# A long convolution with a gated block behind it: the order of the last chunks of the fourth stage, and when two half loads go out

## The chip, the cores and the metric

The kernel runs on 1 core of a Trainium2 chip, all in float32. The metric is device time in microseconds (us) of one launch, the median of several runs. Engines are named as in the profile: PE (TensorE, with PEld its weight loads), DVE (VectorE), ACT (ScalarE), POOL (GpSimd), SP (SyncE, here only a DMA queue).

## The reference, cut to what matters

```python
# x (8, 6400, 128), h (6400, 128); _attn_ref, then _moe_ref on its result
L = 2 * S
y = np.fft.irfft(np.fft.rfft(x, n=L, axis=1) * np.fft.rfft(h, n=L, axis=0)[None], n=L, axis=1)[:, :S]
xp = np.concatenate([np.zeros((B, K - 1, D)), y], axis=1)              # K = 5 taps
gate_pre = sum(conv_w[k] * xp[:, k:k + S] for k in range(K))
out = (1 / (1 + np.exp(-gate_pre))) * (y @ w_val) @ w_out
```

So: a causal convolution of length 6400 for each of 128 channels, then a gate from a 5-tap filter of its result, a product with a projection, and a second projection.

## The kernel before, in words

The long convolution is done by transforms written as matrix products. For each of the 8 batches there are four stages (matmuls are counted as the trace has them, two for each in the code). The first (`Forward`) makes sums and differences of the input on POOL (`sums`, two instructions of 128x256) and multiplies them (`half`, 32 matmuls into two banks of PSUM, which ACT copies away). The second (`Product`) transforms on and multiplies with the spectrum of h, which is loaded in blocks from DRAM into four buffers `h_sb`. The third (`s3_quads`, here s3(g)) has 16 groups g of 64 matmuls; ACT copies part of the result (`keep`, `ends`) and DVE joins it into the tile `dt` with two instructions (`join`). The fourth (`Chunk.s4`) makes the convolution's result in 13 chunks of the 64 columns; a chunk is named by its first column: 60 (four columns), 0, 5, ... 55 (five each).

Batches overlap. The third stage of batch b runs with the first stage of batch b + 1 and with what is left of the chunks of batch b - 1; the fourth stage of batch b runs with the second stage of batch b + 1. The order on every engine is the program's own (`keep_in_program_order`), so an instruction that waits holds all that stand behind it on its engine.

What a chunk c does, under the names of this document:

- s4(c): 40 matmuls into one of four banks of PSUM (`single`; the pool `ps1` has four). The planner gives a bank that is free to the next tile that asks, the one that was freed longest ago; a tile asks when its first matmul comes.
- y(c): an ACT copy of the chunk to SBUF. "Late" chunks (25 to 55 where a batch follows) do nothing else here: their bank is free behind that copy, and their filter is done in the next third stage.
- The other chunks (0, 5, 10, 15, 20) do their filter now, from the bank: `init` and `keep` on ACT, then taps(c) on DVE (taps 0, 1 and 2, each adds into five columns, c + j to c + j + 4; some in two pieces), and add(c) on POOL, which adds the buffer that `keep` filled to columns c + 3 to c + 7. The bank is free when taps(c) are done.
- project(c) (PE), the sigmoid (ACT), gate(c) (DVE), output(c) (PE), store: for 0 and 5 in the fourth stage, for the others in the third stage of the next batch, in the groups that `VALUE` and `OUTPUT` name, late chunks' taps in groups 2k and 2k + 1 with k = (c - 25) / 5.

The fourth stage is a loop over steps s; step s emits, in this order, project of the jobs that are due, s4 of chunk number s, output of the jobs of the step before, ACT's copies for chunk number s, the taps of chunk number s - 1, the add of chunk number s - 2, and the gate of the jobs:

```python
            if 0 < s <= NCH and not cs[s - 1].late:
                cs[s - 1].taps()
            if 2 < s < NCH + 2 and not cs[s - 2].late:
                cs[s - 2].add()
            for c in jobs[s]:
                c.gate()
```

and in steps 9 and 10 of all batches but the last two the first two `sums` of the next first stage (sums(0) and sums(1)); group g of the third stage then emits s3(g), half(g), sums(g + 2), and what is due of the chunks. The second stage has ended on PE by step 8, so steps 9 to 12 hold the last four chunks alone; this document calls them the tail.

Before, the chunks go 60, 0, 35, 40, 45, 50, 55, 5, 10, 15, 20, 25, 30. The buffers that `keep` fills are four, `keeps`: two tiles `p_t` and the two halves of `h_sb[0]`, the latter for chunks 15 and 20 (and for 5). The first block of the spectrum for the next second stage is loaded into the same two halves, on ACT's queue, from the third stage (`ahead`, in the groups that `AHEAD` names); such a load must wait until the add that reads the half is done.

Of the kernel before, what the change touches and what calls it, by code (L numbers as in the profile page):

```python
# [30 lines left out]
CH = 5  # L31
HEAD = (60, 4)
CHUNKS = [HEAD] + [(a, CH) for a in range(0, 60, CH)]
NCH = len(CHUNKS)
OUT_ORDER = CHUNKS[1:] + [HEAD]
LATE = 35
HELD = 10
# [6 lines left out]
XH = 8  # L44
VALUE = {10: 0, 15: 1, 20: 2, 25: 4, 30: 5, 35: 6, 40: 8, 45: 10, 50: 12, 55: 14}
OUTPUT = {10: 2, 15: 3, 20: 4, 25: 6, 30: 7, 35: 8, 40: 9, 45: 11, 50: 13}
AHEAD = {
    0: (1, 0, 0), 1: (1, 0, 1), 4: (0, 0, 0), 5: (0, 0, 1), 7: (1, 1, 0), 8: (0, 1, 0),
    9: (0, 1, 1), 10: (0, 2, 0), 11: (0, 2, 1), 12: (1, 1, 1), 13: (1, 2, 0), 14: (1, 2, 1),
}  # L50

# [78 lines left out]
def longconv_moe(ctx: ExitStack, tc: tile.TileContext, x, h, r1, m2, r3, m4, w64, out):  # L130
# [34 lines left out]
    p_t = [cp.tile([128, CH, N1], F32, name=f"p_{i}") for i in range(2)]  # L165
    keeps = p_t + [h_sb[0][:, i : i + CH * N1].rearrange("p (n t) -> p n t", t=N1) for i in (0, BL // 2)]
# [70 lines left out]
    def single():  # L237
        return ps1.tile([128, 512], F32, name="pt1", tag="pt1")
# [66 lines left out]
    def ahead(spectrum, kb, half):  # L305
        i = half * SB // 2
        if spectrum:
            k = slice(2 * C * i, 2 * C * i + SB * C)
            nc.scalar.dma_start(h_sb[kb % HB][:, k], hd[kb, :, k])
        else:  # L310
            j = kb * SB + i
            nc.scalar.dma_start(m2_sb[kb % M2B][:, i : i + SB // 2], m2[:, j : j + SB // 2])
# [58 lines left out]
    def s3_quads(d0):  # L371
        pt = pair()
        for q in range(4):
            for c in range(2):
                for r, k in ((0, 0), (1, 0), (1, 1), (0, 1)):
                    d, o = k * HP + d0 + q, (r + k) % 2
                    w = d // 2 * 2 * N1 + c * 2 * HR + d % 2
                    v = pt[o * HP : (o + 1) * HP, k, q * 2 * N2 : (q + 1) * 2 * N2].rearrange("p (b m) -> p b m", b=2)
                    nc.tensor.matmul(
                        v[:, :, c::2],  # L380
                        lhsT=gyf[r * HP : (r + 1) * HP, w : w + 2 * HP - 1 : 2],
                        rhs=r3_sb[r * HP : (r + 1) * HP, c, :],
                        start=True,
                        stop=True,
                    )
        v = pt.rearrange("p k (d b m) -> p b m k d", b=2, m=N2)
        a = d0 // 4 % 2 * 512
        t = h_sb[HB - 1][:, a : a + 512]
        o = dv.rearrange("p n c (k d) -> p (n c) k d", k=2)[:, :, :, d0 : d0 + 4]

        def keep():
            act(
                t.rearrange("p (m c d) -> p m c d", c=2, d=2 * XG)[:, :, ::-1],
                pt.rearrange("p k (d b m c) -> p b m c (k d)", b=2, m=N2 // 2, c=2)[:, 1],
            )

        def join(op, n):
            u = t.rearrange("p (m k d) -> p m k d", k=2, d=XG)
            nc.vector.tensor_tensor(out=n, in0=v[:, 0, 2:], in1=u[:, 2:], op=op)

        def ends():
            act(o[:, 0:2], v[:, 0, :2])
            act(o[:, N2 : N2 + 2], v[:, 1, :2])

        return keep, ends, lambda: join(ADD, o[:, 2:N2]), lambda: join(ALU.subtract, o[:, : N2 + 1 : -1])
# [26 lines left out]
    class Chunk:  # L432
# [51 lines left out]
                self.p = self.y  # L484

        def keep(self):
            self.q = p_t[(self.ch[0] - HELD) // CH % 2] if self.late else keeps[(self.i + (self.i // 8 if self.defer else 1)) % 4]
            self.first(3, self.q, self.p)
            if self.r is not None:
                self.first(2, self.r, self.p)  # L490
# [95 lines left out]
    def m4_load(j, half=None):  # L586
        a = CH * j, CH * j + CH + (j == 12)
        if half is not None:
            a = (a[0] + 2 * half, a[1] if half else a[0] + 2)
        a = slice(*a)  # L590
        nc.sync.dma_start(m4_sb[:, a], m4.rearrange("k (n t) -> k n t", t=MW)[:, a])
# [28 lines left out]
    for b in range(B):  # L620
        nxt = b + 1 < B


        steps = collections.defaultdict(list)
        for c in pend:
            a = c.ch[0]
            if a == HEAD[0]:
                t = NS - 1
            else:
                t = VALUE[a]  # L630
            if c.late:
                k = (a - WAIT) // CH
                if not nxt:
                    c.r = rows[k % 3]
                steps[2 * k] += [lambda c=c: c.taps(range(2))]
                steps[2 * k + 1] += [lambda c=c: c.taps(range(2, 4)), c.add]
            steps[t] += [c.project]
            steps[t if a in OUTPUT else NS - 1] += [c.sigm, c.gate]
            if a in OUTPUT:
                steps[OUTPUT[a]] += [c.output]  # L640
                steps[OUTPUT[a] + 1] += [c.store]
        pend = [c for c in pend if c.ch[0] in (HEAD[0], HEAD[0] - CH)]
        for g in range(NS):
            e = s3_quads(4 * g)
            f = []
            if nxt:
                f = fx.half([single(), single()])
                fx.sums(nc.gpsimd)
            for u in e:
                u()  # L650
            if nxt and g in AHEAD:
                ahead(*AHEAD[g])
            for u in f:
                u(act)
            if b == 0:
                next(wgen, None)
                next(wgen, None)
                if g < 8:
                    m4_load(m4_rest[0], g % 2)
                    if g % 2:  # L660
                        m4_rest.pop(0)
            for u in steps[g]:
                u()
        if nxt:
            h_load(HB - 1)
        if b + 2 < B:
            fx = Forward(x[b + 2], gy)


        chs = CHUNKS if not nxt else sorted(CHUNKS, key=lambda c: (c != HEAD, c[0] > 0, c[0] < LATE))  # L670
        cs = [Chunk(b, i, ch, nxt) for i, ch in enumerate(chs)]
        jobs = collections.defaultdict(list)
        for i, c in enumerate(cs):
            if i and not c.late and not c.held:
                jobs[i + 3].append(c)
        if not nxt:
            jobs[NCH + 2].append(cs[0])
        pr = {}

        def s2(kb):  # L680
            if nxt and kb < NKB:
                pr[kb] = Product(kb)
                m2_load(kb + M2B)

        def times(kb):
            if kb in pr:
                pr[kb].mul_u()
                pr[kb].mul_t()
                pr.pop(kb).add()
                h_load(kb + HB)  # L690

        outs, at = [], 0
        for s in range(max(NCH, *jobs) + 2):
            kbs = list(range(at, min(at + 2 - s % 2, NKB))) if nxt else []
            at += len(kbs)
            if s == 0:
                s2(0)
                s2(1)
            if s < 2:
                cs[s].s4()  # L700
            late = pend[s : s + 1]
            if late and s == 0:
                late[0].output()
            for kb in kbs[:1]:
                if kb:
                    s2(kb + 1)
            if m4_rest:
                m4_load(m4_rest.pop(0))
            for c in jobs[s]:
                c.project()  # L710
            if 1 < s < NCH:
                cs[s].s4()
            for c in outs + late[: s]:
                c.output()
            for c in jobs[s]:
                c.sigm()
            for kb in kbs[:1]:
                times(kb)
            for kb in kbs[1:]:
                s2(kb + 1)  # L720
            if s < NCH:
                cs[s].copies()
            for c in outs + late:
                c.store(p_t[0][:, : c.ch[1]] if s == 0 or nxt and c.ch[0] == CH else None)
            for kb in kbs[1:]:
                times(kb)
# [6 lines that stand above are left out]
            outs = jobs[s]  # L733
            if b + 2 < B:
                if s == 5:
                    fx.load(XB)
                if s in (9, 10):
                    fx.sums(nc.gpsimd)
        pend = [cs[0]] + [c for c in cs if c.held or c.late]
# [45 lines left out]
```

## Time and profile before

| | |
|---|---|
| median of 3 runs | 947.44 us (945.7 to 949.0) |
| the profiled execution | 948.98 us, its span 947.2 us |
| PE, DVE, POOL, ACT busy | 861.0, 746.1, 580.3, 511.4 us |
| mean granted clock of PE | 0.986 |
| one period (third and fourth stage) | about 108 us |

The span runs from the first to the last instruction on the core; the time holds some 1.8 us around it. Busy time is the union of an engine's instructions. There are seven seams from a fourth to a third stage where a batch follows (at 201, 309, 416, 524, 635, 742 and 851 us); the change touches each of them. The last fourth stage, at 893 us, keeps its order.

### The profile page before, as it was taken

The numbers are of one execution on the slowest core, as the hardware profiler recorded it, in microseconds if no ns is written. First come the engines' busy times: TensorE is split into PE (matmuls) and PEld (weight loads), VectorE is DVE, ScalarE is ACT, GpSimd is POOL, SyncE is SP. The second block draws the span as 40 slices with busy tenths as digits, with TensorE's granted clock in tenths as the row PEclk, the third lists the DMA queues.
The fourth block names the chain that finished last, engine by engine and source line by source line (L and its number), as shares of the span: only waits on it lengthen the run. The fifth ranks groups of instructions, "written<-read, shape, count | busy, mean of one in ns | idle before, by whom it ended". The sixth has DMA issues, their size and how long they took to land. (4 is left out here: it accounts for less than half of the span.)

```text
span 947.2 us, 48024 instructions
## 1 busy us (share of the span) xinstructions
PE 861.0 (91%) x21360; PEld 687.3 (73%) x21360; DVE 746.1 (79%) x1041; ACT 511.4 (54%) x1222; POOL 580.3 (61%) x602
## 2 busy tenths in 40 slices
PE   7799668998999999999899989999999898999897
PEld 6699658965688658975688657875589666985563
DVE  5546757887898879888797867879888787979785
ACT  4522443277624784178624765157733685248776
POOL 5446744776477765867477754876558664764332
PEclk9899799999999999999999999999999999999999
DMA  7776646926584566925594455935576365921112
GB/s 251 261 256 240 205 153 233 341 81 174 171 312 156 152 199 204 317 82 175 168 307 155 131 188 173 334 105 160 178 266 234 104 200 153 316 92 47 66 56 96
DMA packets 79406, 177.42 MB, mean 187 GB/s; under 512 B 14048, under 2 KB 27360, under 8 KB 79200
## 3 DMA queue, kind: packets, MB, share of 16 engines
q1 hardware_dynamic: 67104, 152.33, 48.0%
q10 hardware_dynamic: 12096, 22.03, 8.0%
q8 instruction: 168, 2.75, 1.2%
q14 instruction: 38, 0.31, 0.1%
HBM read 141.56 MB, written 32.77 MB: 184 GB/s over the span
## 5 line engine op out<-in xcount | busy, mean ns | idle before, releaser
L117 POOL TENSOR_TENSOR gy<-gy,ring 128x512 f32<-128x512 f32 (+1 forms) x182 | 220.6, 1244 | 104.5 <-DVE ring L117 52.4
L117 PEld LDWEIGHTS pt<-r_sb,gy 64*64 64x64 f32 x8192 | 143.8, 138 | 105.2 <-issue 66.9
L117 DVE TENSOR_TENSOR dt<-pt,ring 128x496 f32<-128x496 f32 x256 | 159.8, 667 | 66.3 <-ACT dt L117 63.2
L117 PEld LDWEIGHTS pt<-m_sb,dt 128*64 128x64 f32 x4096 | 184.8, 136 | 28.8 <-issue 12.7
L117 POOL TENSOR_TENSOR sd<-x 128x256 f32<-128x256 f32 x236 | 183.3, 806 | 28.2 <-issue 13.4
L117 PE MATMUL pt<-m_sb,dt 128*64 128x100 f32 x4096 | 192.6, 248 | 7.7 <-DVE ring L117 6.4
L117 PE MATMUL pt<-gy,ring 128*64 128x128 f32 x3008 | 187.3, 278 | 9.2 <-PE pt L117 4.2
L117 ACT COPY ring<-pt 128x512 f32<-128x512 f32 (+2 forms) x216 | 129.2, 601 | 119.6 <-PE pt L117 58.9
L117 PEld LDWEIGHTS pt<-gy,ring 128*64 128x64 f32 x3008 | 174.5, 135 | 21.4 <-PE pt L117 8.0
L117 PE MATMUL pt<-r_sb,gy 64*64 64x64 f32 x8192 | 163.2, 227 | 17.5 <-issue 12.2
L117 PE MATMUL pt<-r_sb,sd 50*64 50x100 f32 x4608 | 144.8, 260 | 33.3 <-issue 25.8
L117 DVE TENSOR_TENSOR gy<-pt,ring 128x1024 f32<-128x1024 f32 (+1 forms) x99 | 117.0, 1182 | 52.5 <-PE pt L117 50.6
L117 PEld LDWEIGHTS pt<-r_sb,sd 50*64 50x64 f32 x4608 | 120.3, 142 | 39.6 <-issue 29.8
L117 DVE TENSOR_TENSOR ring<-pt,ring 128x1024 f32<-128x1024 f32 (+2 forms) x131 | 134.6, 1028 | 11.3 <-PE pt L117 2.4
L117 ACT COPY gy<-pt 128x400 f32<-128x400 f32 x248 | 110.6, 500 | 36.3 <-PE pt L117 35.1
L117 ACT COPY yl<-pt 128x500 f32<-128x500 f32 (+1 forms) x89 | 51.2, 575 | 125.8 <-PE pt L117 125.7
L117 POOL TENSOR_TENSOR gl<-gl,p 128x500 f32<-128x500 f32 (+1 forms) x46 | 54.1, 1177 | 105.9 <-DVE gl L117 69.4
L117 ACT COPY dt<-pt 128x16 f32<-128x16 f32 (+2 forms) x310 | 62.7, 254 | 72.8 <-PE pt L117 72.7
L117 DVE SCALAR_TENSOR_TENSOR gl<-yl,w_sb,gl 128x500 f32<-128x500 f32 (+1 forms) x107 | 91.9, 864 | 3.1 <-ACT gl L117 1.1
L117 PE MATMUL pt<-ring,w_sb 128*64 128x500 f32 x320 | 81.5, 604 | 3.2 <-DVE ring L117 3.1
L117 DVE SCALAR_TENSOR_TENSOR ring<-pt,w_sb,ring 128x500 f32<-128x500 f32 (+3 forms) x94 | 63.1, 671 | 5.7 <-ACT ring L117 1.3
L117 POOL TENSOR_TENSOR ring<-ring,p 128x500 f32<-128x500 f32 (+1 forms) x24 | 25.2, 1051 | 46.8 <-DVE ring L117 22.8
(62 smaller groups left out, 795.5 us busy)
## 6 DMA issues: line engine op xcount, KB each, us to landing
ring<-m SPq DMA_DIRECT2D x69, 512.0 KB, 5.8
ring<-hd SPq DMA_DIRECT2D x63, 512.0 KB, 5.1
x<-xl SPq DMA_DIRECT2D x118, 256.0 KB, 3.5
ring<-hd ACTq DMA_DIRECT2D x42, 256.0 KB, 3.3
ring<-m ACTq DMA_DIRECT2D x42, 256.0 KB, 3.8
out<-ring SPq DMA_DIRECT2D x40, 250.0 KB, 3.9
out<-yl SPq DMA_DIRECT2D x40, 250.0 KB, 4.0
hd<-ring SPq DMA_DIRECT2D x8, 512.0 KB, 4.1
```

What stands on the lines that cost most here:

```text
L117: return self._tc.keep_in_program_order(call(*args, **kwargs))
```

## The change: another order of six chunks, and two loads two groups later

The order of the chunks becomes 60, 0, 35, 40, 45, 50, 55, 5, 10, 25, 15, 20, 30, written out as `ORDER`: the late chunk 25 moves ahead of 15 and 20. The buffers of `keep`, which went by a chunk's number in the order, are written out by its column (`KEEP`). The two half loads of the spectrum's first block move from groups 0 and 1 of the third stage to groups 2 and 3. As the rest of a chunk's work goes through the list in the new order, chunk 25 also comes before 15 and 20 in each group of the third stage.

```diff
+ORDER = (60, 0, 35, 40, 45, 50, 55, 5, 10, 25, 15, 20, 30)
+KEEP = {0: 1, 5: 3, 10: 1, 15: 2, 20: 3}
 AHEAD = {
-    0: (1, 0, 0), 1: (1, 0, 1), 4: (0, 0, 0), 5: (0, 0, 1), 7: (1, 1, 0), 8: (0, 1, 0),
+    2: (1, 0, 0), 3: (1, 0, 1), 4: (0, 0, 0), 5: (0, 0, 1), 7: (1, 1, 0), 8: (0, 1, 0),
     9: (0, 1, 1), 10: (0, 2, 0), 11: (0, 2, 1), 12: (1, 1, 1), 13: (1, 2, 0), 14: (1, 2, 1),
 }
...
         def keep(self):
-            self.q = p_t[(self.ch[0] - HELD) // CH % 2] if self.late else keeps[(self.i + (self.i // 8 if self.defer else 1)) % 4]
+            a = self.ch[0]
+            if self.late:
+                self.q = p_t[(a - HELD) // CH % 2]
+            else:
+                self.q = keeps[KEEP[a] if self.defer else (self.i + 1) % 4]
...
-        chs = CHUNKS if not nxt else sorted(CHUNKS, key=lambda c: (c != HEAD, c[0] > 0, c[0] < LATE))
+        chs = CHUNKS if not nxt else [(a, CH) if a < HEAD[0] else HEAD for a in ORDER]
```

## Rows read from the trace of the kernel before

**Rows 1.** The page, part 1: busy time, share of the span and instructions of each engine.

```profile
PE 861.0 (91%) x21360; PEld 687.3 (73%) x21360; DVE 746.1 (79%) x1041; ACT 511.4 (54%) x1222; POOL 580.3 (61%) x602
```

**Rows 2.** Busy time in one fourth stage (first row) and the third stage behind it: stretch, its length, then busy time (and instructions) of PE, PEld, DVE, ACT, POOL, the granted clock, the DMA share and GB/s.

```profile
148.05:201.45 53.40, 49.90 (x933) 46.63 (x933) 45.05 (x56) 17.47 (x31) 38.65 (x37) 1.00 0.70 250
201.45:255.92 54.47, 50.63 (x1618) 32.71 (x1616) 43.87 (x65) 42.39 (x115) 32.86 (x38) 1.00 0.55 166
```

**Rows 3.** The timeline of PE at the end of the first batch's fourth stage and in the first groups of the next third stage: start, duration, engine, line, operation, out<-in, count, and in brackets the idle time before it and what ended that. The first row holds s4(5), s4(10) and s4(15); then project(5), s4(20), s4(25), output(5), s4(30), s3(0), half(0), project(10); after the dots half(2), and s3(3).

```profile
187.00 5.33 PE L117 MATMUL pt<-m_sb,dt 128*64 128x100 f32 x120
192.17 1.01 PE L117 MATMUL pt<-dt,w_sb 128*64 128x500 f32 x4
193.41 1.94 PE L117 MATMUL pt<-m_sb,dt 128*64 128x100 f32 x40 [0.23 <-DVE ring L117]
195.83 1.94 PE L117 MATMUL pt<-m_sb,dt 128*64 128x100 f32 x40 [0.48 <-DVE ring L117]
198.74 1.06 PE L117 MATMUL pt<-dt,w_sb 128*64 128x500 f32 x4 [0.97 <-DVE dt L117]
199.63 1.89 PE L117 MATMUL pt<-m_sb,dt 128*64 128x100 f32 x40
201.45 1.19 PE L117 MATMUL pt<-r_sb,gy 64*64 64x64 f32 x64
202.45 0.87 PE L117 MATMUL pt<-r_sb,sd 50*64 50x100 f32 x32
203.25 1.06 PE L117 MATMUL pt<-ring,w_sb 128*64 128x500 f32 x4
...
208.25 0.90 PE L117 MATMUL pt<-r_sb,sd 50*64 50x100 f32 x32
...
210.91 1.34 PE L117 MATMUL pt<-r_sb,gy 64*64 64x64 f32 x64
```

**Rows 4.** The timeline of PE, the same output(5) in the seventh and last of these tails.

```profile
848.58 1.06 PE L117 MATMUL pt<-dt,w_sb 128*64 128x500 f32 x4 [0.98 <-DVE dt L117]
```

**Rows 5.** The timeline of DVE over the stretch of rows 3: the last tap of chunk 10, taps(15), gate(5), taps(20), join(0) (two instructions), and the first of the late taps of chunk 25, which reads two operands from SBUF.

```profile
194.94 0.74 DVE L117 SCALAR_TENSOR_TENSOR ring<-pt,w_sb,ring 128x500 f32<-128x500 f32 x1
195.81 2.28 DVE L117 SCALAR_TENSOR_TENSOR ring<-pt,w_sb,ring 128x500 f32<-128x500 f32 x3
198.02 0.67 DVE L117 TENSOR_TENSOR dt<-pt,dt 128x500 f32<-128x500 f32 x1
198.60 2.28 DVE L117 SCALAR_TENSOR_TENSOR ring<-pt,w_sb,ring 128x500 f32<-128x500 f32 x3
203.47 1.26 DVE L117 TENSOR_TENSOR dt<-pt,ring 128x496 f32<-128x496 f32 x2 [2.59 <-ACT dt L117]
...
205.49 1.30 DVE L117 SCALAR_TENSOR_TENSOR ring<-ring,w_sb 128x500 f32<-128x500 f32 x1
```

**Rows 6.** The timeline of POOL over the same stretch: the second half of add(5), sums(0), add(10), sums(1), add(15) with add(20), and sums(2) with sums(3).

```profile
195.76 0.83 POOL L117 TENSOR_TENSOR ring<-ring 128x300 f32<-128x300 f32 x1 [2.06 <-DVE ring L117]
196.54 1.43 POOL L117 TENSOR_TENSOR sd<-x 128x256 f32<-128x256 f32 x2
198.24 1.25 POOL L117 TENSOR_TENSOR ring<-ring,p 128x500 f32<-128x500 f32 x1 [0.28 <-DVE ring L117]
199.45 1.42 POOL L117 TENSOR_TENSOR sd<-x 128x256 f32<-128x256 f32 x2
201.02 2.47 POOL L117 TENSOR_TENSOR ring<-ring 128x500 f32<-128x500 f32 x2
203.44 2.82 POOL L117 TENSOR_TENSOR sd<-x 128x256 f32<-128x256 f32 x4
```

**Rows 7.** The timeline of ACT: y(15), and the two copies that empty the banks of half(0).

```profile
192.43 0.58 ACT L117 COPY ring<-pt 128x500 f32<-128x500 f32 x1
...
203.39 0.89 ACT L117 COPY gy<-pt 128x400 f32<-128x400 f32 x2
```

**Rows 8.** The timeline of DVE and POOL in group 3 of the same third stage: a late tap that reads two operands from SBUF, and one instruction of sums beside it.

```profile
211.70 0.91 DVE L117 SCALAR_TENSOR_TENSOR ring<-ring,w_sb 128x500 f32<-128x500 f32 x1
212.01 1.18 POOL L117 TENSOR_TENSOR sd<-x 128x256 f32<-128x256 f32 x1
```

**Rows 9.** The timeline of PE at its longest waits: one in the first batch's third stage, one in a later third stage and the two groups of instructions after it, one in another.

```profile
121.37 0.33 PE L117 MATMUL pt<-r_sb,sd 50*64 50x100 f32 x2 [2.58 <-issue]
...
548.05 0.39 PE L117 MATMUL pt<-r_sb,sd 50*64 50x100 f32 x3 [1.77 <-issue]
549.53 1.89 PE L117 MATMUL pt<-ring,w_sb 128*64 128x500 f32 x4
551.35 1.62 PE L117 MATMUL pt<-r_sb,gy 64*64 64x64 f32 x64
...
788.04 0.24 PE L117 MATMUL pt<-r_sb,sd 50*64 50x100 f32 x1 [1.85 <-issue]
```

**Rows 10.** Busy time in short stretches right behind the three waits of rows 9, columns as in rows 2; the number behind POOL's is the granted clock.

```profile
122.00:124.00 2.00, 2.00 (x80) 2.00 (x74) 0.24 (x1) 1.36 (x5) 1.25 (x2) 0.57 0.05 11
...
549.00:550.00 1.00, 1.00 (x5) 0.24 (x2) 0.09 (x1) 1.00 (x3) 0.98 (x2) 0.50 0.77 240
...
789.00:790.00 1.00, 1.00 (x54) 0.80 (x54) 0.00 (x0) 1.00 (x3) 0.93 (x2) 1.00 0.06 16
```

**Rows 11.** The page, part 6: the DMA issues that the change moves (half blocks of the spectrum): count, KB each, median us from issue to landing.

```profile
ring<-hd ACTq DMA_DIRECT2D x42, 256.0 KB, 3.3
```
## The prediction

> **What bounds the kernel.** I began with the busy shares of the page: PE stands at 91% [rows 1], so any stretch in which PE runs on without a wait is bound by it, and the others matter where they make it wait. The table by stage says how full it is around the change: 49.9 of 53.4 us in a fourth stage, 50.6 of 54.5 in the third stage behind it, with DVE near 44 to 45 in both [rows 2]. Both stages are PE-bound with DVE close behind. The reader is to see that the change can pay only where PE waits, and that DVE's slack, 8 to 11 us a stage, is all that stands between it and PE.
>
> Then I read PE's timeline at the seam. The order of matmuls is fixed by hand, so each bracket is a real hold-up. Three stand there: 0.23 us before s4(20), 0.48 before s4(25), 0.97 before output(5) [rows 3]. The last tail has the third at 0.98 [rows 4]. DVE's timeline tells why: from the last tap of chunk 10 on it has no gap until taps(20) end at 200.88, and gate(5), which output(5) needs, stands behind taps(15) [rows 5]. Then PE is free of it: DVE idles 2.59 us before join(0), waiting for s3(0) and ACT [rows 5]. POOL's timeline comes last, because add(c) writes cells that taps(c+5) also write [rows 6].
>
> **The change, part by part.** Times are those of the first tail, each from its row.
>
> PE gains first. s4(25) now follows s4(10); its bank is freed by the one ACT copy that ends at 192.43 + 0.58 = 193.01 [rows 7], so s4(15) need not wait for taps(5). project(5) leaves PE at about 193.1, a chunk takes 201.45 - 199.63 = 1.82 [rows 3], so s4(15) 193.1, s4(20) 194.9, output(5) 196.75. gate(5) has nothing before it but taps(10), which end at 195.68 [rows 5], so it is done at 196.4 and holds nothing. output(5) 0.89, s4(30) 1.82: s3(0) starts at 199.45, not 201.45. **PE gains 2.0 us**, which is the three waits (1.68) and the pipeline's drain ahead of them. If the bank of taps(5) is handed out instead, 0.3 less.
>
> DVE and POOL lose. Before, taps(15) precede add(10) in the program and POOL waits (0.28 us [rows 6]). Now chunk 25 has no taps in its step, so add(10), on cells 13 to 17, precedes taps(15), on cells 15 to 21, and **DVE must wait for POOL**. POOL's queue there: add(5) at 195.76 (it waits for taps(10), as before), sums(0) at 196.54, which take 1.38 to the next start, so add(10) at 197.92, 1.25 long, done at 199.17 [rows 6]. taps(15) start at 199.3 where they started at 195.81: 3.5 late. They take 2.28, then 0.13 as between the last tap of chunk 10 and taps(15) (195.81 - 195.68), and taps(20) take 2.28 [rows 5]: 201.72 to 204.0, 3.1 later than before. Queued behind them on DVE is join(0), which starts at 203.95 instead of 203.47. add(15) and add(20), which touch the cells of taps(20), start at 204.15 instead of 201.02 and end 2.47 later, at 206.6; queued behind them on POOL are sums(2), which start 3.1 later than the 203.44 of before [rows 6].
>
> Who waits for sums(2)? half(2). PE with its 2.0 us gained comes to it early: s3(0) 199.45, half(0) 200.45, project(10) at 201.3. That last wants a bank; those of chunks 15 and 20 are held by their taps, and half(0)'s own are emptied by ACT only 1.8 us behind its start, at 202.3 [rows 7]; so it takes the one that taps(15) free at 201.6, and starts at 201.75. At the pace of before (s3 1.0, half 0.8, project 1.0 [rows 3]) half(2) is reached at 206.35. sums(2) are two instructions of 0.74 less 0.05 of overlap (2.82 for four [rows 6]): from 206.57 to 208.0 if nothing disturbs them. So half(2) starts at 208.1 at best, against 208.25 before [rows 3]: **of 2.0 us gained, 0.15 is left.**
>
> Something may disturb them. The late taps of chunk 25 need add(20), so they now start together with sums(2). Side by side these two kinds stretch: such a tap took 1.30 and 0.91, an instruction of sums 1.18, against 0.74 when sums run alone [rows 5, 6, 8]. One stretch of 1.18 - 0.74 = 0.44 puts half(2) at 208.55, 0.3 behind the old time. Bounds: 0.15 gained, 0.3 lost; I take 0.25 lost, nearer the rows of such pairs. The Trainium skill (SBUF — State Buffer, "SBUF: two separate sides") calls the port that VectorE and GpSimd share an exclusive lock, held for a whole instruction, against a VectorE instruction with two SBUF inputs. By that rule sums(2) lose a whole 0.74, half(2) starts at 208.85, and the sum below has 0.6 for 0.25. The rows show less than a whole instruction lost (0.44 of 0.74), so they decide; with 0.6 the sum would be 7.6.
>
> Behind half(2) DVE is some 1.6 us late, but not on the path. The two late taps of chunk 25 begin at 206.75, behind add(20), where they began at 205.49; at 1.30 and about 1.05 they end at 209.1, and join(1), 1.26 long, at 210.35 [rows 5]. s3(3) needs join(1) by about 211.15 (210.91 [rows 3] plus 0.25): a margin of 0.8. Six of the seven tails have sums in them; the seventh has none, so its add(10) ends 1.4 earlier, but add(20) there still ends near 205.2, and the late taps of chunk 25 start as before: what PE gains goes back, nought.
>
> The rest costs nothing as long as its cover holds. The two half loads go out with the same instructions two groups later, still some 48 us before their block is needed, and land in 3.3 [rows 11]; in groups 0 and 1 they would now have held ACT until add(15) and add(20) end at 205.4 and 206.6, so moving them saves that stall rather than makes one. In the third stage chunk 25 stands ahead of 15 and 20: its third tap goes ahead of gate(15) and delays it by 0.74, with output(15) two groups off; project(25) goes ahead of output(20), same matmuls. KEEP names the buffers that the old rule gave.
>
> **The clock.** PE now stands still in one piece from 206.35 to 208.1 or 208.55: **1.75 to 2.2 us**, where before it ran. What follows such a wait is in the rows: after 2.58 us and after 1.77 the granted clock fell to half (0.57 and 0.50 right behind), after 1.85 it didn't [rows 9, 10]. Half is 1.2 of 2.4 GHz, and dear: four matmuls of an output or project took 1.82 to the next start against 0.89, an s3 1.62 against 1.19 [rows 3, 9]; that is 1.35 in these two, and with what ran slow on either side I put a fall at 1.6. With 2 or 3 falls in six tails that is 4 us.
>
> Sum: 6 x 0.25 + 2.5 x 1.6 = 5.5 us. The profiled execution took 948.98 us (span 947.2), so 954.5 by it; it stands 1.5 above the median of 947.44, so **953 us** in the median.
>
> **The rivals.**
> (a) *The same chain, but the clock holds.* For it: the wait of 1.85, and a wait that PE's own jitter cuts in two. Then 6 times -0.15 to +0.3: 946.5 to 949.2.
> (b) *Faster: taps(15) don't wait for add(10).* If POOL got to add(10) right after taps(10), or didn't have to precede taps(15), these would start when ACT's copies of chunk 15 are there, near 196.7; taps(20) would end by 201.3 and sums(2) as early as before. PE would keep 1.1 to 2.0 us at each seam: 7 times that is 933 to 940. It decides from the point where add(10) ends before 198.5 rather than at 199.17. Against it: the 0.28 us that POOL waits for taps(15) in the old order [rows 6], which shows that these cells are kept in order. A part of it (an add earlier by 0.5) gives 944.
> (c) *Slower through DVE.* The 1.6 us by which DVE is late use up the margin of 0.8, by a few more stretched pairs as in rows 8: then s3(3) or a bank freed by a gate holds PE, 1.0 us more per tail, six times 6: 953 to 959, and 962 with falls of the clock. For it: DVE is busy 43.9 of 54.5 [rows 2], most of it early in the stage.
>
> **How the numbers follow.** Forecast (falls at some seams, 949.5 to 958) 0.50; (a) 0.25; (c) 0.15; (b) 0.10. About 0.3%, 2.8 us, is what a measurement of this kernel can tell from no change (its three runs lie within 945.7 to 949.0). Slower by more: 0.50 less the case of a single fall, plus (c): 0.62. Within: (a) and the rest of the first: 0.28. Faster: (b), 0.10. The range leaves (b) and the top of (c) out: 945.5 to 960; the forecast's own is 949.5 to 958.
>
> **What would show it.** Right: no PE wait between project(5) and s3(0) in the new tail; s4(25) third; DVE idle near 2.9 us before taps(15), released by POOL; add(15) some 3 us later against add(5) than before; a wait of PE before half(2), released by POOL's sums, in six tails and not in the seventh; third stages that begin 2 us earlier and last 2 to 4 longer; a granted clock of 0.5 behind some of these waits. Wrong: taps(15) right behind gate(5) (then (b)); PE waiting on DVE's join or gate in groups 3 to 6 (then (c)); no wait before half(2).

## The result and the profile after

The changed kernel takes **951.74 us** in the median (948.88 to 953.01), the kernel before, run beside it, 947.47 (942.93 to 954.02). The ratio is 1.0052, with a 95% interval of 1.0035 to 1.007: slower by half a per cent, 3.3 to 6.6 us. The time, the direction and the main mechanism came out as forecast; two terms of the sum did not, and by luck they made up for each other.

The busy shares, in part 1 of the page of the changed kernel, are those of [rows 1], but for 8 us of POOL: its `sums` stretch beside more of DVE's work. The work is the same; what moved is who waits.

```profile
PE 860.9 (91%) x21360; PEld 687.7 (73%) x21360; DVE 746.6 (79%) x1041; ACT 511.2 (54%) x1222; POOL 588.0 (62%) x602
```

PE's timeline at the first seam, which answers to [rows 3]. It holds project(5); s4(15) with s4(20); output(5); s4(30); s3(0); half(0); project(10); after the dots half(2), output(10), project(20) and s3(3). This kernel's helper is line 119 where it was 117.

```profile
191.92 1.01 PE L119 MATMUL pt<-dt,w_sb 128*64 128x500 f32 x4
193.16 3.65 PE L119 MATMUL pt<-m_sb,dt 128*64 128x100 f32 x80 [0.23 <-DVE ring L119]
196.62 1.02 PE L119 MATMUL pt<-dt,w_sb 128*64 128x500 f32 x4
197.46 1.91 PE L119 MATMUL pt<-m_sb,dt 128*64 128x100 f32 x40
199.30 1.19 PE L119 MATMUL pt<-r_sb,gy 64*64 64x64 f32 x64
201.39 0.92 PE L119 MATMUL pt<-r_sb,sd 50*64 50x100 f32 x32 [0.90 <-DVE ring L119]
202.24 1.06 PE L119 MATMUL pt<-ring,w_sb 128*64 128x500 f32 x4
...
208.15 0.92 PE L119 MATMUL pt<-r_sb,sd 50*64 50x100 f32 x32 [0.92 <-POOL sd L119]
209.00 1.06 PE L119 MATMUL pt<-ring,w_sb 128*64 128x500 f32 x4
211.09 1.06 PE L119 MATMUL pt<-ring,w_sb 128*64 128x500 f32 x4 [1.03 <-DVE ring L119]
212.08 1.19 PE L119 MATMUL pt<-r_sb,gy 64*64 64x64 f32 x64
```

This profile reaches the seam 0.25 us earlier (191.92 against 192.17), so stretches are counted from project(5). The reader is to see three waits of about 1 us where [rows 3] have none: before half(0), half(2) and project(20). Five of the seven seams show all three. At the fourth the one before half(2) is missing (below), and the last third stage, which has no `half`, has a single wait, before s3(3), for DVE's join:

```profile
858.99 1.19 PE L119 MATMUL pt<-r_sb,gy 64*64 64x64 f32 x64 [1.14 <-DVE dt L119]
```

At the first seam s3(0) comes 7.38 us behind project(5), where it came 9.28 behind; but s3(3) comes 20.16 behind it, where it came 18.74 behind. PE gains 1.9 us in the tail and is 1.42 late at s3(3).

DVE's timeline of the same stretch, which answers to [rows 5]: gate(5), taps(15) with taps(20), join(0); after the dots two late taps of chunk 25; then its third tap and gate(15).

```profile
195.35 0.67 DVE L119 TENSOR_TENSOR dt<-pt,dt 128x500 f32<-128x500 f32 x1
198.96 4.71 DVE L119 SCALAR_TENSOR_TENSOR ring<-pt,w_sb,ring 128x500 f32<-128x500 f32 x6 [2.94 <-POOL ring L119]
203.58 1.25 DVE L119 TENSOR_TENSOR dt<-pt,ring 128x496 f32<-128x496 f32 x2
...
206.32 2.31 DVE L119 SCALAR_TENSOR_TENSOR ring<-ring,w_sb 128x500 f32<-128x500 f32 x2 [0.92 <-POOL ring L119]
...
209.72 0.72 DVE L119 SCALAR_TENSOR_TENSOR ring<-ring,w_sb 128x500 f32<-128x500 f32 x1
210.37 0.67 DVE L119 TENSOR_TENSOR ring<-pt,ring 128x500 f32<-128x500 f32 x1
```

POOL's, which answers to [rows 6]: the second half of add(5), sums(0), add(10), then add(15) with add(20), and sums(2) with sums(3).

```profile
195.51 0.83 POOL L119 TENSOR_TENSOR ring<-ring 128x300 f32<-128x300 f32 x1 [2.06 <-DVE ring L119]
196.29 1.42 POOL L119 TENSOR_TENSOR sd<-x 128x256 f32<-128x256 f32 x2
197.67 1.25 POOL L119 TENSOR_TENSOR ring<-ring,p 128x500 f32<-128x500 f32 x1
...
203.81 2.48 POOL L119 TENSOR_TENSOR ring<-ring 128x500 f32<-128x500 f32 x2 [3.50 <-ACT ring L119]
206.24 3.67 POOL L119 TENSOR_TENSOR sd<-x 128x256 f32<-128x256 f32 x4
```

The chain is to be read across the two: add(10) ends at 197.67 + 1.25 = 198.92, and at 198.96 DVE ends its 2.94 us of idling and starts taps(15). Everything behind them is about 3 us late: add(15) and add(20), and behind those sums(2), which half(2) waits for. And gate(15) ends at 211.04, 0.05 before project(20) starts: project(20) takes the bank of project(15), which that gate frees.

The granted clock at the seams, in windows with the columns of [rows 2] (the number behind POOL's is the clock), the first and the last of seven; the five between show 1.00 too.

```profile
199.30:214.00 14.70, 11.84 (x404) 7.86 (x404) 13.37 (x20) 10.00 (x27) 10.52 (x12) 1.00 0.33 106
...
850.50:866.00 15.50, 14.36 (x419) 8.17 (x416) 13.95 (x23) 12.83 (x33) 7.75 (x8) 1.00 0.11 37
```

It never fell at a seam.

### The profile page after: what moved, and what is told of

It is laid out like the page before. It is cut to its first block, busy times and chain, and to the rows that moved or that the text cites. A ratio compares the mean times of both kernels' runs of the same rounds, so it can differ in the third digit from the quotient of the medians.

```text
span 947.9 us, 48025 instructions
## 1 busy us (share of the span) xinstructions
PE 860.9 (91%) x21360; PEld 687.7 (73%) x21360; DVE 746.6 (79%) x1041; ACT 511.2 (54%) x1222; POOL 588.0 (62%) x602
## 5 line engine op out<-in xcount | busy, mean ns | idle before, releaser
L119 POOL TENSOR_TENSOR sd<-x 128x256 f32<-128x256 f32 x236 | 190.9, 838 | 28.9 <-issue 13.6
L119 PE MATMUL pt<-ring,w_sb 128*64 128x500 f32 x320 | 82.0, 600 | 10.2 <-DVE ring L119 10.1
L119 POOL TENSOR_TENSOR ring<-ring 128x500 f32<-128x500 f32 (+1 forms) x24 | 26.5, 1116 | 45.8 <-ACT ring L119 25.8
```

What stands on the lines that cost most here:

```text
L119: return self._tc.keep_in_program_order(call(*args, **kwargs))
```

## The experiments

The theory after the result: the loss is the order of add(10) and taps(15). Because add(10) stands ahead, DVE idles, and PE pays in pieces, partly through banks that DVE frees late. The rivals: the third stage's order (25 ahead of 15 and 20 in each group) costs the time, through project(20)'s bank; or the loads do. Each ratio is against the kernel before, run on the same chip beside it.

**Add(10) one step later, behind taps(15).** All else as changed.

```diff
+        adds = collections.defaultdict(list)
+        for i, c in enumerate(cs):
+            if i and not c.late:
+                adds[i + (3 if nxt and c.ch[0] == HELD else 2)].append(c)
...
-            if 2 < s < NCH + 2 and not cs[s - 2].late:
-                cs[s - 2].add()
+            for c in adds[s]:
+                c.add()
```

> The changed kernel with add(10) emitted one step later, behind taps(15) as in the old order. Theory (DVE's wait of 2.94 us for add(10) makes taps(15), taps(20), add(15), add(20) and sums(2) late, and PE then waits three times for 0.9 to 1.0 us): taps(15) start some 2.3 us earlier in the tail, none of the three waits of PE is left or only the last in part, and PE keeps 1.1 to 2.0 us at each of seven seams against the kernel before: 933 to 940 us. Rival (the loss is made in the third stage, by chunk 25 standing ahead of 15 and 20 there): the wait of project(20) on gate(15) stays at about 1 us, and the time stays within 3 us of the changed kernel, 949 to 955.

937.84 us, ratio 0.9921 (0.9893 to 0.995). DVE's timeline, taps(15) with taps(20), and the late taps of chunk 25:

```profile
196.96 4.71 DVE L119 SCALAR_TENSOR_TENSOR ring<-pt,w_sb,ring 128x500 f32<-128x500 f32 x6 [0.87 <-ACT ring L119]
...
204.31 2.32 DVE L119 SCALAR_TENSOR_TENSOR ring<-ring,w_sb 128x500 f32<-128x500 f32 x2 [0.88 <-POOL ring L119]
```

PE's timeline, half(2) and project(20):

```profile
206.15 0.92 PE L119 MATMUL pt<-r_sb,sd 50*64 50x100 f32 x32
...
209.10 1.06 PE L119 MATMUL pt<-ring,w_sb 128*64 128x500 f32 x4 [1.04 <-DVE ring L119]
```

taps(15) now wait for ACT's copy alone, and start 2.0 us earlier. The waits before half(0) and half(2) are gone, while project(20) still waits 1.04 here (and at two seams more): that one was expected to go or to shrink, and it did neither. So the place of one POOL instruction decides the sign: between this kernel and the changed one lie 1.0052 - 0.9921 = 1.3%, some 12 us, and the new order of the chunks (with the loads moved), freed of this wait, is worth 0.8%, 7.5 us.

**The third stage in column order.** Chunks 15 and 20 stand ahead of 25 in each group again.

```diff
-        pend = [cs[0]] + [c for c in cs if c.held or c.late]
+        pend = [cs[0]] + sorted((c for c in cs if c.held or c.late), key=lambda c: (c.ch[0] < LATE, c.ch[0]))
```

> The changed kernel, but the rest of the chunks goes through the third stage by column again (10, 15, 20, 25, 30), as before; the tail keeps the new order. Rival (third-stage order): gate(15) stands 0.72 us earlier on DVE, the wait of 1.03 us before project(20) falls to 0.3, six times 0.7 is 4.3: 947 to 948 us, as the kernel before. Theory (the late DVE and POOL of the tail are the cause): the two waits before half(0) and half(2) stay, the one before project(20) shrinks by up to 0.7 or moves to the next s3, the time is 947 to 951.

952.72 us, ratio 1.0093 (1.0059 to 1.0127). PE's timeline, project(20) and project(30):

```profile
211.21 1.06 PE L119 MATMUL pt<-ring,w_sb 128*64 128x500 f32 x4 [0.38 <-DVE ring L119]
...
222.38 1.06 PE L119 MATMUL pt<-ring,w_sb 128*64 128x500 f32 x4 [1.36 <-DVE ring L119]
```

gate(15) is earlier, so project(20) waits 0.38 instead of 1.03; what that gives is lost at project(30), 1.36 where the changed kernel waits 0.83. half(0) and half(2) wait 0.90 and 0.92 as in the changed kernel. The rival falls: the order of the third stage moves a wait from one project to the next, and undoing it gains nothing. The theory's own range, 947 to 951, was missed too: it had not counted the longer wait before project(30). If anything this version is slower than the changed kernel (1.0059 to 1.0127 against 1.0035 to 1.007).

**Both edits together.** Its diff is the two above.

> Both of the first two edits on the changed kernel: add(10) behind taps(15), and the third stage by column. Theory: as the first edit alone or up to 2 us faster, 931 to 940 us. Rival (third-stage order): 947 to 948, as the second edit alone.

935.9 us, 0.9915 (0.9886 to 0.9944): the same as the first edit alone, within the intervals. project(20) waits 0.38, project(30) 1.83. Undoing the order of the third stage gains nothing in either company.

**The two loads alone, on the kernel before.**

```diff
-    0: (1, 0, 0), 1: (1, 0, 1), 4: (0, 0, 0), 5: (0, 0, 1), 7: (1, 1, 0), 8: (0, 1, 0),
+    2: (1, 0, 0), 3: (1, 0, 1), 4: (0, 0, 0), 5: (0, 0, 1), 7: (1, 1, 0), 8: (0, 1, 0),
```

> The kernel before with the second part of the change alone: the two half loads in groups 2 and 3, the chunks in the old order. Theory: no difference that can be measured, 946 to 949 us. Rival (the later loads are what costs): slower by the whole 4 us, 951 to 953, with ACT or the first Product of the next second stage waiting for them.

945.03 us, 0.9997 (0.9964 to 1.0031): nothing, as costed.

**The loads left where they were, in the changed kernel.** The same diff, the other way round.

> The changed kernel with the half loads back in groups 0 and 1, so the first part of the change alone. As predicted: ACT stands at the load of group 0 until add(15) ends (205.1 in the changed kernel's trace) though it comes there at 201.3, so the copies of half(0) and the gate work behind them are 3 to 4 us late, PE 1 to 3 us a seam: 958 to 970 us by a kernel before of 947, that is slower than the changed kernel by 0.7 to 2%. Rival (the load has no part in it): as the changed kernel, 1.005 of the kernel before.

955.39 us, 1.0119 (1.0091 to 1.0146), so 0.7% slower than with the loads moved (a difference of two ratios: 0.3 to 1.0%), the low end of what was expected. ACT's timeline, the two copies that empty the banks of half(0), then PE's, half(1):

```profile
203.19 0.26 ACT L119 COPY dt<-pt 128x16 f32<-128x16 f32 x2
207.60 0.89 ACT L119 COPY gy<-pt 128x400 f32<-128x400 f32 x2 [4.15 <-POOL ring L119]
...
208.15 0.91 PE L119 MATMUL pt<-r_sb,sd 50*64 50x100 f32 x30 [1.42 <-ACT gy L119]
```

The load's issue, on ACT's queue, waits for POOL's adds, as the prediction reckoned, and holds ACT's own copies for 4.15 us; half(1) then waits 1.42 for them. Under this order the loads have to move: moving them is worth nothing alone and 0.7% in company.

**sums(0) and sums(1) one step later.** POOL comes to add(10) earlier by the 1.38 us of sums(0), and the order of add(10) and taps(15) stays.

```diff
-                if s in (9, 10):
+                if s in (10, 11):
                     fx.sums(nc.gpsimd)
```

> The changed kernel, sums(0) and sums(1) emitted one step later, so that add(10) stands ahead of sums(0) on POOL and the wait of DVE is 1.38 us shorter (1.6 of 2.94 left). Theory: the time goes with this wait: of the 1.3% between the changed kernel and the one with add(10) behind taps(15), 1.38 of 2.0 us of earlier taps come back, so 0.996 to 0.998 of the kernel before, and the wait before half(0) is gone. Rival (it is the order of add and taps as such, or a bank, and not how long DVE waits): no change against the changed kernel, 1.005.

938.98 us, 0.996 (0.9938 to 0.9982). DVE's timeline, taps(15) with taps(20):

```profile
200.27 4.70 DVE L119 SCALAR_TENSOR_TENSOR ring<-pt,w_sb,ring 128x500 f32<-128x500 f32 x6 [1.56 <-POOL ring L119]
```

DVE's wait is halved, 2.94 to 1.56. The wait before half(0) is gone, half(2) waits 0.38, and project(20) 1.04 as in the changed kernel. The time follows: 2.94 us of waiting give a ratio of 1.0052, 1.56 give 0.996, and 0.87 (on ACT) 0.9921. That is a dose with its response (the intervals of the last two just overlap), and the edit touched no order in the third stage.

**The first edit, with add(20) ahead of add(15).** In the first experiment the late taps of chunk 25 waited 0.88 for add(20).

```diff
-                adds[i + (3 if nxt and c.ch[0] == HELD else 2)].append(c)
+                adds[i + 2 + (nxt and c.ch[0] in (HELD, 15))].insert(0, c)
```

> add(10) behind taps(15), and add(20) ahead of add(15) on POOL: the wait of 0.88 us of the late taps of chunk 25 for add(20) goes, and DVE is that much earlier at gate(15). Theory (what is left of PE's wait before project(20), 1.04 us, is this wait handed on): that wait falls to 0.2 and the time by 3 to 6 us against add(10) behind taps(15) alone, 0.986 to 0.989 of the kernel before. Rival (DVE is full there and something else takes its place): 0.992, as without it.

932.86 us, **0.9892** (0.9866 to 0.9917): the lowest of all, and clear of both kernels. Its lead over the first experiment (0.9893 to 0.995) is not clear of the noise. PE's timeline, half(2), then output(10) and project(20) in one piece:

```profile
204.39 0.92 PE L119 MATMUL pt<-r_sb,sd 50*64 50x100 f32 x32 [0.42 <-POOL sd L119]
205.24 2.03 PE L119 MATMUL pt<-ring,w_sb 128*64 128x500 f32 x8
```

With DVE 0.88 us earlier, gate(15) frees its bank in time and the wait before project(20) is gone; half(2) and project(30) still wait, 0.42 and 1.24.

**The wait alone, on the kernel before.** The chunks stay in their old order, and add(10) is put ahead of taps(15).

```diff
+            early = nxt and 2 < s < NCH + 2 and cs[s - 2].ch[0] == HELD
+            if early:
+                cs[s - 2].add()
             if 0 < s <= NCH and not cs[s - 1].late:
                 cs[s - 1].taps()
-            if 2 < s < NCH + 2 and not cs[s - 2].late:
+            if 2 < s < NCH + 2 and not cs[s - 2].late and not early:
                 cs[s - 2].add()
```

> The kernel before, its old order of chunks and loads, with the new wait alone: add(10) is emitted ahead of taps(15). Theory: taps(15) start 3.5 us late, gate(5) and output(5) behind them too, PE's wait of 0.97 grows to 4.4 in six seams (3.0 in the seventh): 15 to 24 us slower, 1.016 to 1.025, and up to 1.037 if the granted clock falls behind these waits. Rival (DVE's wait is hidden): within 0.5% of the kernel before.

977.17 us, 1.0348 (1.0321 to 1.0374). DVE's timeline, taps(15); then PE's, output(5) and the s4 behind it, and the same output(5) at the last seam:

```profile
201.41 2.29 DVE L117 SCALAR_TENSOR_TENSOR ring<-pt,w_sb,ring 128x500 f32<-128x500 f32 x3 [3.50 <-POOL ring L117]
...
204.42 1.93 PE L117 MATMUL pt<-dt,w_sb 128*64 128x500 f32 x4 [4.43 <-DVE dt L117]
206.12 2.60 PE L117 MATMUL pt<-m_sb,dt 128*64 128x100 f32 x40
...
879.20 1.20 PE L117 MATMUL pt<-dt,w_sb 128*64 128x500 f32 x4 [3.08 <-DVE dt L117]
```

Windows right behind that wait, the first and the last of seven, columns as above:

```profile
204.50:207.90 3.40, 3.40 (x30) 2.26 (x32) 1.90 (x3) 0.57 (x1) 1.29 (x2) 0.55 0.11 41
...
880.30:883.70 3.40, 3.40 (x50) 3.26 (x50) 0.91 (x2) 0.61 (x2) 2.33 (x2) 0.54 0.20 75
```

Here gate(5) stands behind taps(15), so output(5) takes DVE's whole delay: PE stands 4.43 us in one piece at six seams and 3.08 at the last, and the granted clock is 0.52 to 0.55 in the windows behind it at all seven. By rows, the first seam loses 4.43 - 0.97 = 3.46 in the wait, and 1.93 - 1.06 + 2.60 - 1.89 = 1.58 in the two pieces that run slow behind it, near the 1.6 at which the prediction put a fall of the clock. Other seams lose more behind the wait: s3(0) comes 5.0 to 6.0 us later behind project(5) than in the kernel before at the first six and 3.8 at the last; less the growth of the wait, 3.46 and 2.10, that leaves 1.5 to 2.5 for a fall. The seven sum to 37 us, and the time shows 33 (0.0348 of 942.81).

Behind project(5), taps(15) start 3.4 us later here than in the kernel before, for 33 us; in the new order they start 2.1 us later in the changed kernel than in the first experiment, for 12. So a microsecond of this lateness costs nearly 10 us in the old order of the chunks and 6 in the new one.

## Why the prediction came out, point by point

**PE's gain: right.** 1.9 us against 2.0, the same at all seven seams (7.38 to 7.40 us from project(5) to s3(0)). The 0.3 that I had left open came as the remaining 0.23 before s4(15): the bank of taps(5) was handed out.

**DVE's wait for add(10): right.** 2.94 against 2.9, released by POOL; add(15) and add(20) at 203.81 + 0.25 = 204.06 against 204.15; sums(2) at 206.49 against 206.57; half(2) at 208.40, between my two bounds of 208.1 and 208.55 (the 0.25 brings this profile to the time of the one before). The first experiment shows that this wait is the cause, and the sixth that the loss goes with its size.

**The loads: right.** Moving them costs nothing alone, and the stall that it avoids is real. Undoing the order of the third stage gains nothing either, but not for the reason that I gave (below).

**The stretch of sums: a little under-sized, without effect.** Beside the late taps of chunk 25, sums(2) and (3) took 3.67 us for four instructions, where four took 2.82 [rows 6]: 0.85 more, near two of the 0.44 that I allowed one of. By the lock that the Trainium skill describes (SBUF — State Buffer, "Terms", the shared port pair: the loser is blocked for the whole instruction) each of two instructions would have lost up to 0.74, by estimate 1.48; the trace shows less than that, 0.85 in all. half(2) itself was within the bounds.

**The step that failed is the bank of half(0).** I gave half(0) a free bank, gave that of taps(15) to project(10) with 0.45 us of waiting, and let PE run into one wait of 1.75 to 2.2 us before half(2). But half(0) got the bank of taps(15), the ones that end late: they end at 201.24, half(0) starts at 201.39, and PE stood 0.90 us there and reached half(2) with only 0.92 left to wait. The sum had a slip as well: from project(10) at 201.75, at the pace written there, half(2) is reached at 206.55 and not at 206.35, so the long wait would have been 1.55 to 2.0 us, in part below the 1.77 that is the shortest with a fall in [rows 9, 10]. Two terms came out wrong, in opposite directions:

- *The clock: 4 us forecast, none seen at the seams.* Behind waits of 0.90, 0.92 and 1.03 us, and behind the 1.14 us of the last seam, the granted clock stayed at 1.00. The mechanism exists (the last experiment has it at each seam, behind 4.43 and 3.08 us), but its condition, a long wait in one piece, never came about. For such a wait the forecast's 2 or 3 falls in six were fair: in the ten traces, behind the first batch, the clock fell behind six of ten single waits of 1.77 to 1.86 us. What failed is that PE would have such a wait at all. So of the prediction's signs the clock of 0.5 showed at no seam, and the wait before half(2) at five of six.
- *What a seam loses: 0.25 forecast at half(2), 1.42 measured at s3(3) of the first seam, 0.97 in the mean of six (below).* I had DVE's lateness behind half(2) off the path, by a margin of 0.8 that I took against join(1), and the 0.74 that chunk 25's third tap adds to gate(15) at nothing, "with output(15) two groups off". But gate(15) has a nearer reader: it frees the bank of project(15), which project(20) takes one group later, and holds it 1.03 us. This is rival (c)'s mechanism, a bank freed by a gate, at the 1.0 us priced there. A margin has to be taken against every tile that waits for an instruction, the one that only wants its bank among them.

Six seams of 1.42 would be 8.5 us, and the time shows 3.3 to 6.6. **The first seam is not the mean.** In the changed kernel s3(3) comes 20.14 to 20.17 us behind project(5) at all six; in the kernel before it comes 18.74, 18.77, 18.54, 19.12, 19.05 and 20.93 behind, 19.19 in the mean. So a seam loses 0.97, six lose 5.8, and with the 0.4 that the seventh gains it is 5.4, which the measured time bears out. What spreads the kernel before are waits of PE that the trace puts down to nothing it shows ("issue"). Its sixth seam has two ahead of s3(3):

```profile
747.32 0.91 PE L117 MATMUL pt<-r_sb,sd 50*64 50x100 f32 x29 [0.80 <-issue]
...
751.87 0.38 PE L117 MATMUL pt<-r_sb,sd 50*64 50x100 f32 x2 [0.85 <-issue]
```

The changed kernel has one there, at its fourth seam, in half(1); after the dots half(2):

```profile
529.48 0.39 PE L119 MATMUL pt<-r_sb,sd 50*64 50x100 f32 x3 [0.67 <-issue]
...
531.85 0.92 PE L119 MATMUL pt<-r_sb,sd 50*64 50x100 f32 x32
```

It costs nothing: PE comes later to half(2), doesn't wait for sums(2) any more, and s3(3) stands at 20.16 as ever. Such waits are also fewer behind another wait: up to s3(3) of the six seams they sum to 1.9 to 2.8 us in the six traces in which PE doesn't wait before half(0) (the kernel before has 2.2), and to 0 to 0.7 in the three in which it does and in the last experiment, where it has just stood for 4.43. That is one execution of each kernel, and why it is so is not shown.

The same count, six times the mean shift of s3(3) against the kernel before and the shift of the last period, gives -7.4 us for the first experiment (measured 7.5 faster), -11.1 for add(20) first (10.2 faster) and +33.9 for the last experiment (33 slower). It fails for the column order, +1.4 against 8.8, whose wait has moved behind s3(3), to project(30).

The waits of PE over the whole trace by what ended them, of the kernel before and of the changed one (total us, count, longest):

```profile
PE pt L117 <- issue: 38.0, 41, 3.5
PE pt L117 <- DVE ring L117: 10.6, 21, 1.7
PE pt L117 <- DVE dt L117: 9.0, 10, 1.3
```

```profile
PE pt L119 <- issue: 32.0, 33, 2.9
PE pt L119 <- DVE ring L119: 21.2, 30, 1.4
PE pt L119 <- POOL sd L119: 4.6, 5, 0.9
PE pt L119 <- DVE dt L119: 3.1, 4, 1.4
```

The waits on DVE's `dt` are mostly those before output(5) and are gone, and those on `ring` and on `sd` are the new ones. "issue" is 6 us less, most of it behind s3(3), where it varies between single executions. So these two traces differ by 0.8 us only, where the medians differ by 4.3: over the six periods the kernel before loses 4.5 us more behind s3(3), and about 4 of these lie in one stretch, from s3(3) to s3(8) behind the fourth seam, 21.1 us against 17.0, with the wait of 1.77 us and the slow clock of [rows 9, 10].

**The seventh seam: right in the time.** Without sums there, from project(5) to the end of the span it is 105.2 us before and 104.8 after. Most of what PE gains goes back at DVE's join: PE waits 1.14 us for it before s3(3).

So the forecast of 953 us lies 1.3 above the median, with a sum of 5.5 us against 4.3 measured, through two errors that all but cancel: no fall of the clock (4 us too much), and a seam that is dearer by a bank (0.7 us too little, six times). That the number is so near is luck; that the change loses, and through add(10), is not.

**The rival on the faster side** was not this kernel, but its condition was the right one: "taps(15) don't wait for add(10)" came true in the first experiment, with 0.9921, 7.5 us, where 7 times 1.1 to 2.0 were reckoned. It falls just short of the low end, as project(20) and project(30) still wait for DVE.

## What to carry to other kernels

Moving a piece of work in a hand-ordered queue can turn an instruction that followed into one that must be waited for: look at every pair that writes the same cells, and ask for each engine which of the two now stands first; here one POOL add put back behind the taps turned +0.5% into -0.8%; another, taken ahead of its neighbour, gave -1.1%, which is not clear of -0.8. When an engine becomes late, follow each bank that it frees to the tile that will ask next, since that decides whether PE waits once for long or several times for a little. Measure a loss at every seam of the trace, and not at the first alone: here they were 1.42 and 0.97. And a reordering should be tried with the later order of its dependants redone as well, for a moved chunk may be worth it although the change as made is not.

## What the runs showed of the hardware

Waits of PE at one seam don't add up for the granted clock. Three of 0.90, 0.92 and 1.03 us, 2.85 in sum, left it at 1.00 at every seam that has them. One of 3.08 us, and one of 4.43 at six more seams, left it at 0.52 to 0.55 in the windows behind, and a fall cost 1.5 to 2.5 us.

In between it goes either way. Of ten single waits of 1.77 to 1.86 us in the ten traces (both kernels and eight experiments), behind the first batch, six were followed by a fall. Two of the ten stand before project(30) at two seams of one trace, that of both edits together; PE's timeline at the two, then windows with the columns as above:

```profile
221.54 1.86 PE L119 MATMUL pt<-ring,w_sb 128*64 128x500 f32 x4 [1.83 <-DVE ring L119]
...
646.42 1.06 PE L119 MATMUL pt<-ring,w_sb 128*64 128x500 f32 x4 [1.86 <-DVE ring L119]
```

```profile
221.60:225.00 3.40, 3.40 (x66) 1.83 (x69) 2.38 (x4) 0.05 (x1) 2.13 (x3) 0.51 0.73 172
646.40:649.80 3.40, 3.38 (x104) 2.19 (x106) 2.69 (x5) 1.20 (x6) 2.14 (x3) 1.00 0.86 221
```

The four matmuls take 1.86 us behind the first and 1.06 behind the second. In the first batch of the same trace a single wait of 3.07 us left the clock at 1.00. So the length of a wait alone doesn't decide it, and a forecast can give such falls a chance, not a time.

Lateness of DVE cost nearly 10 us for each microsecond in the old order of the chunks and 6 in the new one. The falls of the clock are a part of it; the other part is that PE there took the whole delay, and in the new order had other work to do meanwhile.

A wait of PE that the trace puts down to nothing is not added to one that the schedule makes: at the fourth seam of the changed kernel 0.67 us of it took the place of the wait before half(2), and s3(3) came when it came at the others.
